# A mixture of experts behind linear attention: routing weights on POOL, and eight routing operations per evacuation

## The chip, the cores and the metric

The kernel runs on one core of one Trainium2 chip. The metric is device time in microseconds (us) of one execution. Engines are called by the profile's names: PE (TensorE), with PEld for its weight loads, DVE (VectorE), ACT (ScalarE), POOL (GpSimd) and SP (SyncE, which only issues transfers here).

## The reference

Two stages. The first is causal linear attention with a decay `lam` per head (batch 4, 8 heads, 768 positions, head size 64), in blocks. Its output is laid out as 3072 tokens of 512 numbers, `x`. The second is a noisy top-2 mixture of 8 experts, cut here to what matters:

```python
logits = x @ w_gate
noise_scale = np.log1p(np.exp(x @ w_noise))
noisy_logits = logits + noise_scale * noise
top2 = np.argpartition(-noisy_logits, 2, axis=1)[:, :2]
top2_l = np.take_along_axis(noisy_logits, top2, axis=1)
top2_l = top2_l - top2_l.max(-1, keepdims=True)
top2_w = np.exp(top2_l)
top2_w /= top2_w.sum(-1, keepdims=True) + 1e-09
for e in range(E):
    for k in range(2):
        mask = top2[:, k] == e
        h = np.maximum(x[mask] @ w1[e], 0.0)
        out[mask] += top2_w[mask, k, None] * (h @ w2[e])
```

So each token has two chosen experts and two weights that sum to one: with `a` the difference of its two largest logits and `e = exp(-a)`, they are 1/(1+e) and e/(1+e).

## The kernel before, in words

**Attention** is a loop of 12 steps `t`, each two chunks of 128 positions of all heads. A step transposes the next step's keys and queries (`trans_k`, `trans_q`), updates the state (`kv`), forms the output (`intra`, `inter`), evacuates it (`evac_o`) and makes the next step's scores (`scores`, whose products DVE masks at L337). `kdecay`, two multiplications on POOL (L322), prepares the keys of step t + 2. One step later the output is multiplied with the gate weights (`products`, L396), stored to `x_tok` in DRAM (`store_x`), and turned into logits (`logits`).

**Routing** is done for three groups of 8 chunks (1024 tokens each). For group `b`, `gate(b)` computes the noisy logits on DVE, the two largest per token (`mx`, L460), their places and a 0/1 matrix `ob` (L472). `weights(b)` fills `rec`, for each token and choice the token's number and its weight; its exponential is a polynomial in `exp_neg` (L92 to L113). `places(b)` counts with PE how many tokens before this one chose the same expert (`count`, L505 to L515, 16 small matmuls on `ob`) and `route(b)` makes of it on DVE the row in the expert's list (`dest`); for the third group `make_order` also ranks the experts. Then 16 scatters per group (`scatter_list`, L548, one per chunk and choice, each 128 rows of 8 bytes) write `rec` into the lists `lst` in DRAM from POOL's queue, each behind a one-element memset (L547).

These are Python generators: every `yield` ends one operation, and the calls `advance(n)` in the loops put up to n operations of the routing at hand between other work; a yielded `"step"` ends such a call early. In attention a step has `advance(4)` behind the query transposes and `advance(16)`, or 10 where it also splits weights, near its end, behind `scatter(SPS)`, which issues up to four of the scatters that are due. The first group's routing is begun at t = 4, the second's at t = 8. At t = 8 `finish(0)` issues what is left of the first group. At t = 10 all scatters left of the first group are issued, then the load of the first list's records (L724) and two gathers of rows of `x_tok` (L728), all on POOL's queue and behind `advance`. After the loop `finish(1)` does the same for the second group, behind the first layer's first block.

**Experts.** Every matmul is done in three products of high and low parts. Expert 0 is worked in three parts of 2, 2 and 3 tiles of 128 tokens (`PARTS0`), so that its first part needs the first group's lists alone, its second the first two groups', its third all. A part is transposes of the gathered rows (`trans_rows`, L737), the first layer in 8 blocks `f` of 12 matmuls (`mm1`, L753), each evacuated by ACT (L759) and DVE (L763), and the second layer, 24 matmuls of 512 columns per tile (`gemm2`, L791). In the first part the loop over `f` calls `advance(FILL1)` after each block, for the third group: f = 0 and 1, whose matmuls were issued earlier, call it too. `advance(50)` follows, up to the `"step"`. `gemm2` of the first tile calls `order_rest`, which is `finish(2)`, before its matmul number `MID`: it issues the rest of the third group's routing, its counts on PE among it, and its 16 scatters. At f = 3 two gathers for the second part stand in POOL's queue; they need the second group's list. The lists and gathers of the third part and of expert 1 follow at the second part's first layer. Experts 1 to 7 run in the order that the counts gave, with their weights loaded (`load_w`) and split (`split_w`, L692 and L693) beside the work of the one before.

A POOL instruction waits in order: what stands behind it in POOL's queue, `kdecay`, scatters and gathers, waits too. The same holds for each of the other engines.

Of the kernel before, what the change touches and what calls it, by code (L numbers as in the profile page):

```python
# [21 lines left out]
FT = mybir.dt.float32  # L22
# [5 lines left out]
OP = mybir.AluOpType  # L28
# [29 lines left out]
MAXOV = 40  # L58
MAXT = 24
FILLA, FILLB = 16, 4  # L60
FILL1 = 5
LOADS = {0: (1, 0), 1: (1, 1), 2: (1, 2), 3: (1, 3), 4: (2, 0), 5: (2, 1), 6: (2, 2), 7: (2, 3)}
SPLITS = {2: (1, 0), 3: (1, 1), 4: (1, 2), 5: (1, 3), 6: (2, 0), 7: (2, 1), 8: (2, 2)}
MID = 16
X1 = ((), (0,), (1,), (2,), (3,), (4,), (5, 6))
WARM = (14, 4, 4, 10)
GX = 10
# [21 lines left out]
    return bass.AP(tensor=ap.tensor, offset=ap.offset + offset, ap=dims)  # L89


def exp_neg(nc, pool, out, a, shape, tag):  # L92

    v = nc.vector
    n = pool.tile(shape, FT, name=tag + "n")
    u = pool.tile(shape, FT, name=tag + "u")
    acc = pool.tile(shape, FT, name=tag + "acc")
    p2 = pool.tile(shape, I32, name=tag + "p2")
    v.tensor_scalar(n, a, -1.0 / math.log(2.0), MAGIC, op0=OP.mult, op1=OP.add)
    yield  # L100
    v.tensor_scalar(n, n, -MAGIC, None, op0=OP.add)
    yield
    v.scalar_tensor_tensor(u, n, math.log(2.0), a, op0=OP.mult, op1=OP.add)
    yield
    v.tensor_scalar(p2, n, 127.0, float(1 << 23), op0=OP.add, op1=OP.mult)
    yield
    v.tensor_scalar(acc, u, EXPC[-1], None, op0=OP.mult)
    yield
    for c in EXPC[-2::-1]:
        v.scalar_tensor_tensor(acc, acc, c, u, op0=OP.add, op1=OP.mult)  # L110
        yield
    v.scalar_tensor_tensor(out, acc, 1.0, p2.bitcast(FT), op0=OP.add, op1=OP.mult)
    yield  # L113


@with_exitstack
def kernel(
# [3 lines left out]
    nc = tc.nc  # L121
# [68 lines left out]
    for i in range(7):  # L190
        n = 1 << i
# [232 lines left out]
    def gate(b):  # L424
        v = nc.vector
        gs = GB[b + 1] - GB[b]
        sh = [128, gs, E]
        t = lambda sh, nm, dt=FT: rp.tile(sh, dt, name=nm)
        pl = PL[b]
        l2 = t([128, gs, 16], "l2")  # L430
        v.tensor_copy(l2, pl[:, :gs, :])
        yield
        zc = t(sh, "zc")
        v.tensor_scalar(zc, l2[:, :, 8:16], 87.0, -87.0, op0=OP.min, op1=OP.max)
        yield
        z = zc.rearrange("p c e -> p (c e)")
        fl = [128, gs * E]
        a = t(fl, "ga")
        v.scalar_tensor_tensor(a, z, -1.0, z, op0=MULT, op1=OP.max)
        yield  # L440
        e = t(fl, "ge")
        yield from exp_neg(nc, rp, e, a, fl, "g")
        acc = t(fl, "glacc")
        v.tensor_scalar(acc, e, LOGC[-1], None, op0=MULT)
        yield
        for c in LOGC[-2::-1]:
            v.scalar_tensor_tensor(acc, acc, c, e, op0=ADD, op1=MULT)
            yield
        acc3 = acc.rearrange("p (c e) -> p c e", e=E)
        v.scalar_tensor_tensor(acc3, l2[:, :, 8:16], 0.0, acc3, op0=OP.max, op1=ADD)  # L450
        yield
        nl = t(sh, "nl")
        v.tensor_mul(nl, acc.rearrange("p (c e) -> p c e", e=E), nz[:, GB[b]:GB[b + 1], :])
        yield
        v.tensor_add(nl, nl, l2[:, :, 0:8])
        yield
        mx = t(sh, "mx")
        mi = t(sh, "mi", U32)
        for c in range(gs):
            v.max(mx[:, c, :], nl[:, c, :])  # L460
            yield
        for c in range(gs):
            v.max_index(mi[:, c, :], mx[:, c, :], nl[:, c, :])
            yield
        ei = t([128, 2, gs], "ei")
        v.tensor_copy(ei.rearrange("p r c -> p c r"), mi[:, :, 0:2])
        yield
        oh = t([128, 2, gs, E], "oh")
        v.tensor_tensor(oh, iota8[:, :, :gs, :], ei[:, :, :, None].to_broadcast([128, 2, gs, E]), op=OP.is_equal)
        yield  # L470
        ob = t(sh, "ob", BF)
        v.tensor_add(ob, oh[:, 0], oh[:, 1])  # L472
        yield
        RT[b] = dict(mx=mx, ei=ei, oh=oh, ob=ob)

    def weights(b):
        v = nc.vector
        gs = GB[b + 1] - GB[b]
        sh = [128, gs, E]
        r = RT[b]  # L480
# [9 lines left out]
        v.tensor_scalar(a, a, 87.0, None, op0=OP.min)  # L490
        yield
        e = t([128, gs], "we")
        yield from exp_neg(nc, rp, e, a, [128, gs], "w")
        s = t([128, gs], "ws")
        v.tensor_scalar(s, e, 1.0, 1e-9, op0=ADD, op1=ADD)
        yield
        v.reciprocal(s, s)
        yield
        recf = rec.bitcast(FT)
        v.tensor_copy(recf[:, :, 0, 1], s)  # L500
        yield
        v.tensor_mul(recf[:, :, 1, 1], e, s)  # L502
        yield

    def count(b):  # L505
        gs = GB[b + 1] - GB[b]
# [67 lines left out]
                                  sub(w, (d * 128 + (h ^ d) * 64) * E, [[E, 64], [256 * E, DB // 2], [1, E]]))  # L574
    keep_warm(WARM[3])

    def merge(*gens):

        gens = list(gens)
        while gens:  # L580
            for x in gens[:]:
                j = next(x, "end")
                if j == "end":
                    gens.remove(x)
                else:
                    yield j

    def places(b):
        yield "step"
        count(b)  # L590
# [3 lines left out]

    def routing(b):
        yield from gate(b)
        yield from merge(weights(b), places(b))
        scatters.extend((b, c, i) for c in range(GB[b + 1] - GB[b]) for i in range(2))
        RT[b]["done"] = True

# [227 lines left out]
    for t in range(NST):  # L828
        u = t + 1
# [278 lines left out]
```

## Time and profile before

| | us |
|---|---|
| three runs | 799.79, 802.74, 807.30 |
| median | 802.74 |
| the profiled execution | 804.76 |
| its span, first to last instruction | 802.9 |
| PE busy | 742.6 (92%), granted clock 0.959 |
| DVE busy | 335.9 (42%) |
| ACT busy | 222.7 (28%) |
| POOL busy | 272.7 (34%) |

The profile has a page and views of one execution's trace. A row of a timeline is: start, duration, engine, line of the kernel, operation, tile written <- tiles read, shape, count, and in brackets how long the engine was idle before it and what ended that. In the row of a group "x48 | 47.2, 982" is 48 instructions, 47.2 us in all, 982 ns each. A row of windows gives a stretch and for each engine its busy time in it with the number of instructions. Spans on POOL are rough. The attention lasts until about 171 us, the first part of expert 0 until about 213, its second until about 250; the rest is the other experts.

### The profile page before, as it was taken

The numbers are of one execution on the slowest core, as the hardware profiler recorded it, in microseconds if no ns is written. First come the engines' busy times: TensorE is split into PE (matmuls) and PEld (weight loads), VectorE is DVE, ScalarE is ACT, GpSimd is POOL, SyncE is SP. The second block draws the span as 40 slices with busy tenths as digits, with TensorE's granted clock in tenths as the row PEclk, the third lists the DMA queues.
The fourth block names the chain that finished last, engine by engine and source line by source line (L and its number), as shares of the span: only waits on it lengthen the run. The fifth ranks groups of instructions, "written<-read, shape, count | busy, mean of one in ns | idle before, by whom it ended". The sixth has DMA issues, their size and how long they took to land. (4 is left out here: it accounts for less than half of the span.)

```text
span 802.9 us, 15437 instructions
## 1 busy us (share of the span) xinstructions
PE 742.6 (92%) x6132; PEld 627.3 (78%) x6132; DVE 335.9 (42%) x796; ACT 222.7 (28%) x381; POOL 272.7 (34%) x399
## 2 busy tenths in 40 slices
PE   5979998784969999999999999999999999999993
PEld 3778877474758889889888888888888888889882
DVE  5435878344412555435243424433352443335210
ACT  0435553232011343214222321322142232214100
POOL 1222115626555145442354234333413433221221
PEclk9899999597979999999999999999999999999997
DMA  7899984111817165344253524333442444240210
GB/s 174 183 279 226 266 231 103 52 56 44 298 50 222 66 172 153 118 145 139 68 144 114 152 82 154 119 118 101 148 133 78 148 134 130 65 129 26 59 53 20
DMA packets 92666, 103.48 MB, mean 129 GB/s; under 512 B 39203, under 2 KB 65315, under 8 KB 92592
## 3 DMA queue, kind: packets, MB, share of 16 engines
q1 hardware_dynamic: 72640, 63.35, 28.8%
q0 software_dynamic: 13136, 36.23, 13.8%
q10 hardware_dynamic: 6816, 2.90, 1.6%
q8 instruction: 49, 0.80, 0.4%
q14 instruction: 25, 0.20, 0.1%
HBM read 77.78 MB, written 25.93 MB: 129 GB/s over the span
## 5 line engine op out<-in xcount | busy, mean ns | idle before, releaser
L753 PE MATMUL pS<-xth,w1h 128*128 128x512 f32 (+3 forms) x544 | 183.6, 338 | 8.5 <-issue 6.3
L753 PE MATMUL pS<-xtl,w1h 128*128 128x512 f32 (+3 forms) x544 | 182.3, 335 | 6.6 <-issue 5.7
L753 PE MATMUL pS<-xth,w1l 128*128 128x512 f32 (+3 forms) x544 | 182.5, 336 | 5.6 <-issue 5.6
L763 DVE SCALAR_TENSOR_TENSOR ht<-pS,ht 128x256 fp32r<-128x256 f32 (+3 forms) x176 | 76.4, 455 | 168.0 <-ACT ht L759 139.5
L810 POOL DMA_INDIRECT out_dram<-ot,rec x46 | 65.3, 1419 | 186.0 <-DVE ot L803 174.8
L791 PE MATMUL pO<-w2h,ht 128*128 128x512 f32 x384 | 126.1, 399 | 0.0
L791 PE MATMUL pKV<-w2h,ht 128*128 128x512 f32 x384 | 125.6, 398 | 0.0
L759 ACT ACTIVATE ht<-pS 128x512 fp32r<-128x512 f32 (+3 forms) x136 | 65.4, 484 | 205.8 <-PE pS L753 159.5
L753 PEld LDWEIGHTS pS<-xth,w1h 128*128 128x128 f32 x544 | 104.4, 192 | 19.0 <-issue 6.4
L753 PEld LDWEIGHTS pS<-xth,w1l 128*128 128x128 f32 x544 | 104.4, 192 | 16.9 <-issue 8.1
L753 PEld LDWEIGHTS pS<-xtl,w1h 128*128 128x128 f32 x544 | 104.4, 192 | 14.4 <-issue 4.4
L739 ACT ACTIVATE xth<-pS 128x512 fp32r<-128x512 f32 (+2 forms) x53 | 29.8, 572 | 205.2 <-PE pS L737 205.0
L791 PEld LDWEIGHTS pO<-w2h,ht 128*128 128x128 f32 x384 | 72.7, 189 | 16.3
L791 PEld LDWEIGHTS pKV<-w2h,ht 128*128 128x128 f32 x384 | 72.3, 188 | 16.3
L791 PE MATMUL pO<-w2l,ht 128*128 128x512 f32 x192 | 76.0, 396 | 0.0
L791 PE MATMUL pKV<-w2l,ht 128*128 128x512 f32 x192 | 75.7, 394 | 0.0
L322 POOL TENSOR_TENSOR kd<-kt,Mk 128x512 f32<-128x512 f32 x24 | 24.8, 1056 | 101.8 <-PE pR L381 57.7
L548 POOL DMA_INDIRECT lst<-rec,dest x48 | 47.2, 982 | 34.6 <-DVE rec L502 24.9
L775 POOL DMA_INDIRECT pv<-out_dram,rec x46 | 47.1, 1025 | 31.0 <-issue 28.0
L728 POOL DMA_INDIRECT xg<-x_tok,rec x46 | 50.1, 1090 | 21.3 <-issue 14.8
L803 DVE SCALAR_TENSOR_TENSOR ot<-pO,rec,pv 128x512 f32<-128x512 f32 x21 | 15.8, 751 | 82.7 <-PE pO L791 82.7
L803 DVE SCALAR_TENSOR_TENSOR ot<-pKV,rec,pv 128x512 f32<-128x512 f32 x21 | 15.8, 751 | 81.4 <-PE pKV L791 81.4
(186 smaller groups left out, 977.1 us busy)
## 6 DMA issues: line engine op xcount, KB each, us to landing
wst<-in_moe_w_dram SPq DMA_DIRECT2D x48, 512.0 KB
wst<-in_moe_w_dram SPq DMA_DIRECT2D x32, 256.0 KB
x_tok<-xc SPq DMA_DIRECT2D x24, 256.0 KB
out_dram<-zero SPq DMA_DIRECT2D x24, 256.0 KB
kt<-in_k_dram SPq DMA_DIRECT2D x11, 512.0 KB
qt<-in_q_dram SPq DMA_DIRECT2D x22, 256.0 KB
vt<-in_v_dram SPq DMA_DIRECT2D x10, 512.0 KB
vt<-in_v_dram ACTq DMA_DIRECT2D x2, 512.0 KB
```

Of the source, the lines that this page charges most:

```text
L322: nc.gpsimd.tensor_mul(kd[:, :, s], kt[:, :, s], mask(s, slice(0, HP), slice(C - 1, C)).to_broadcast([128, HP, 2, D]))
L548: st = nc.gpsimd.indirect_dma_start(out=lst, out_offset=bass.IndirectOffsetOnAxis(ap=r["dest"][:, i, c:c + 1], axis=0), in_=r["rec"][:, c, ...
L728: nc.gpsimd.indirect_dma_start(out=XG[t][:size(e, t)], out_offset=None, in_=x_tok[:rows, :], in_offset=bass.IndirectOffsetOnAxis(ap=REC[e, ...
L739: nc.scalar.activation(hi, p, AF.Copy)
L753: nc.tensor.matmul(p, W1[a][d][:, fs], xt(b, cs)[:, d], start=(d == 0 and i == 0), stop=(d == DB - 1 and i == 2))
L759: nc.scalar.activation(ht(e, 0, f, cs), p, AF.Relu)
L763: nc.vector.scalar_tensor_tensor(ht(e, 1, f, c), p[:, r], 0.0, ht(e, 0, f, c).bitcast(FT), op0=OP.max, op1=SUB)
L775: nc.gpsimd.indirect_dma_start(out=PV[t][:size(e, t), :], out_offset=None, in_=out, in_offset=bass.IndirectOffsetOnAxis(ap=REC[e, t][:, 0: ...
L791: nc.tensor.matmul(p, ht(e, a, f, cs), W2[b][f // 2][:, f % 2, :], start=(i == 0), stop=(i == len(terms) - 1))
L803: nc.vector.scalar_tensor_tensor(o, p, w, pv, op0=MULT, op1=ADD)
L810: st = nc.gpsimd.indirect_dma_start(out=out, out_offset=bass.IndirectOffsetOnAxis(ap=REC[e, t][:, 0:1], axis=0), in_=o, in_offset=None, bo ...
```

## The change

Three things. `weights(b)` is written for POOL instead of DVE, but for the reciprocal, which stays on DVE; POOL has no use of the fused operation with two inputs and a scalar here, so `exp_neg` makes two operations of each such one, in all 25 on POOL for 19 on DVE. `routing` no longer issues weights and places in turn: all of the weights up to the sum are issued at once when the gate is done, then the places, then the reciprocal and the last two operations. And two constants change: `FILL1`, routing operations per block in expert 0's first part, from 5 to 8, and `MID`, the matmul of the first tile's second layer before which `order_rest` is called, from 16 to 6.

```diff
-FILL1 = 5
+FILL1 = 8
...
-MID = 16
+MID = 6
...
-def exp_neg(nc, pool, out, a, shape, tag):
-
-    v = nc.vector
+def exp_neg(v, pool, out, a, shape, tag, fused=True):
+
+    def stt(o, x, c, y, op0, op1):
+        if fused:
+            v.scalar_tensor_tensor(o, x, c, y, op0=op0, op1=op1)
+        else:
+            v.tensor_scalar(o, x, c, None, op0=op0)
+            v.tensor_tensor(o, o, y, op=op1)
+        yield
+
...
-    v.scalar_tensor_tensor(u, n, math.log(2.0), a, op0=OP.mult, op1=OP.add)
-    yield
+    yield from stt(u, n, math.log(2.0), a, OP.mult, OP.add)
...
     for c in EXPC[-2::-1]:
-        v.scalar_tensor_tensor(acc, acc, c, u, op0=OP.add, op1=OP.mult)
-        yield
-    v.scalar_tensor_tensor(out, acc, 1.0, p2.bitcast(FT), op0=OP.add, op1=OP.mult)
-    yield
+        yield from stt(acc, acc, c, u, OP.add, OP.mult)
+    yield from stt(out, acc, 1.0, p2.bitcast(FT), OP.add, OP.mult)
...
-        yield from exp_neg(nc, rp, e, a, fl, "g")
+        yield from exp_neg(v, rp, e, a, fl, "g")
...
     def weights(b):
-        v = nc.vector
+        v = nc.gpsimd
...
-        yield from exp_neg(nc, rp, e, a, [128, gs], "w")
+        yield from exp_neg(v, rp, e, a, [128, gs], "w", fused=False)
         s = t([128, gs], "ws")
         v.tensor_scalar(s, e, 1.0, 1e-9, op0=ADD, op1=ADD)
-        yield
-        v.reciprocal(s, s)
+        yield "sum"
+        nc.vector.reciprocal(s, s)
         yield
         recf = rec.bitcast(FT)
         v.tensor_copy(recf[:, :, 0, 1], s)
-        yield
         v.tensor_mul(recf[:, :, 1, 1], e, s)
-        yield
...
-    def merge(*gens):
-
-        gens = list(gens)
-        while gens:
-            for x in gens[:]:
-                j = next(x, "end")
-                if j == "end":
-                    gens.remove(x)
-                else:
-                    yield j
-
...
     def routing(b):
         yield from gate(b)
-        yield from merge(weights(b), places(b))
+        ws = weights(b)
+        while next(ws) != "sum":
+            pass
+        yield from places(b)
+        yield from ws
         scatters.extend((b, c, i) for c in range(GB[b + 1] - GB[b]) for i in range(2))
         RT[b]["done"] = True
```

## The prediction

> **What bounds the kernel now.** I read the 40 slices of the page first: TensorE (PE) is at 9 tenths in nearly every slice after 260 us, so whatever reaches PE late after that has no room to show, and what is to be won or lost lies where it is thin, at 120 to 160, 180 to 200 and 220 to 240 us. PE's waits over 100 to 245 us (whom it waited for: us in total, times, longest) say of what kind these holes are:
>
> ```profile
> core 0 of [0], span 802.9 us
> ...
> PE pS L753 <- issue: 16.9, 18, 1.8
> PE pS L334 <- issue: 3.2, 6, 1.1
> ...
> PE pS L334 <- DVE qTs L313: 0.8, 1, 0.8
> ```
>
> Hardly any of it is a wait for another engine: "issue" is time in which the profile shows nothing to wait for. The windows (busy time of PE, PEld, DVE, ACT, POOL, then the granted clock, the DMA share and GB/s) put it in place:
>
> ```profile
> 120.00:137.00 17.00, 15.36 (x425) 13.68 (x416) 14.92 (x48) 7.45 (x15) 8.85 (x14) 0.90 0.49 125
> 137.00:154.00 17.00, 11.06 (x66) 4.41 (x59) 3.27 (x12) 0.20 (x1) 12.31 (x23) 0.60 0.03 2
> 154.00:171.00 17.00, 15.26 (x338) 14.16 (x336) 12.37 (x68) 7.99 (x15) 2.74 (x4) 0.90 0.29 97
> 171.00:186.00 15.00, 12.27 (x100) 11.11 (x100) 5.13 (x19) 5.19 (x12) 9.06 (x17) 1.00 0.11 36
> 186.00:198.00 12.00, 2.97 (x12) 2.38 (x12) 3.52 (x14) 0.95 (x3) 7.97 (x15) 0.73 0.02 1
> 198.00:209.00 11.00, 11.00 (x61) 9.34 (x61) 8.73 (x69) 2.82 (x7) 2.21 (x3) 0.82 0.96 340
> 209.00:221.50 12.50, 11.32 (x76) 10.04 (x74) 3.29 (x7) 1.47 (x3) 10.14 (x19) 1.00 0.78 250
> 221.50:232.00 10.50, 3.63 (x13) 2.35 (x13) 0.43 (x1) 0.38 (x1) 6.73 (x13) 0.70 0.02 1
> ```
>
> In 137 to 154, 186 to 198 and 221.5 to 232 us PE gets through 66, 12 and 13 matmuls, DMA moves 1 or 2 GB/s, and POOL is the one engine that works. What POOL does then is its timeline:
>
> ```profile
> 136.65 1.04 POOL L548 DMA_INDIRECT lst<-rec,dest  x1 [0.15 <-issue]
> ...
> 150.75 0.97 POOL L548 DMA_INDIRECT lst<-rec,dest  x1 [0.23 <-issue]
> 154.26 0.59 POOL L724 DMA_DIRECT2D recz<-lst  x1 [2.55 <-DMA lst<-rec,dest]
> 156.37 1.06 POOL L728 DMA_INDIRECT xg<-x_tok,recz  x1 [1.52 <-DMA recz<-lst]
> 157.73 1.01 POOL L728 DMA_INDIRECT xg<-x_tok,recz  x1 [0.30 <-issue]
> 158.74 0.09 POOL L547 MEMSET spacer<- 1x1 f32 x1
> 175.19 1.04 POOL L548 DMA_INDIRECT lst<-rec,dest  x1 [16.36 <-DVE rec L502]
> ...
> 199.52 1.10 POOL L728 DMA_INDIRECT xg<-x_tok,recz  x1 [4.00 <-ACT ht L759]
> ...
> 209.38 1.04 POOL L548 DMA_INDIRECT lst<-rec,dest  x1 [7.34 <-DVE rec L502]
> ```
>
> Each hole is the tail of a run of list scatters: twelve of the first group (136.65 to 151.7, one per 14.10/11 = 1.28 us), sixteen of the second from 175.19, sixteen of the third from 209.38. PE keeps going for some 11 to 12 us of the sixteen and then crawls until about 2.4 us after the last one (175.19 + 16 x 1.28 = 195.6, PE back at 198.0; 209.38 + 20.4 = 229.8, back at 232.0; the twelve: 151.7, back at 153.7). What the crawl is made of the trace doesn't show; that it goes with the scatters, all three times, it does. In 175.2 to 198 PE did 89 matmuls (x100 and x12, less the 23 before 175.2), in 209.4 to 232 some 87. I take it that a run of sixteen lets PE do about 88 and no more, however long these are. The price of a run is then 22.8 us less what 88 matmuls would take, and it matters **when the run starts and which matmuls stand under it.**
>
> **What is waited for in turn.**
>
> ```profile
> 153.72 1.29 DVE L337 TENSOR_TENSOR at<-pS,Mk 128x512 f32<-128x512 f32 x2 [12.10 <-PE pR L396]
> ...
> 156.99 0.64 DVE L460 MAX8 mx<-nl 128x8 f32<-128x8 f32 x8
> ```
>
> ```profile
> 171.77 1.09 PE L737 MATMUL pS<-identf,xg 128*128 128x128 f32 x8
> ...
> 174.65 0.28 PE L753 MATMUL pS<-xth,w1l 128*128 128x256 f32 x1
> 174.77 0.28 PE L753 MATMUL pS<-xth,w1h 128*128 128x256 f32 x1
> ...
> 200.80 0.63 PE L791 MATMUL pO<-w2h,ht 128*128 128x512 f32 x1
> ...
> 212.97 1.03 PE L737 MATMUL pS<-identf,xg 128*128 128x128 f32 x8
> ```
>
> A first-layer matmul of two tiles costs 0.12 us from start to start, the last twelve after the crawl 2.8/12 = 0.23 us (198.0 to 200.80, lower clock), a second-layer one 12.17/48 = 0.25 us with the counts of the third group among them.
>
> **The change, part by part.** Counting yields: `gate` has 45, `weights` had 19, of which 18 vector operations leave DVE per group (the reciprocal stays); POOL gets 25. Of these, two copies need nothing late, 21 form a chain from the maxima (`mx`) to the sum, two follow the reciprocal. All 23 up to the sum are issued at once where the gate ends, ahead of the next scatters.
>
> *Price of the chain.* No such POOL operation is in this trace. Nearest rows:
>
> ```profile
> 1.74 0.19 POOL L234 MEMSET linit<- 128x116 int32 x1
> 1.99 0.15 POOL L235 MEMSET linit<- 128x58 int32 x1
> ...
> L1026 POOL COPY spacer<-ht 1x1 f32<-1x1 f32 x53 | 9.5, 179 | 105.2 <-ACT ht L759 105.1
> ```
>
> The second memset overwrites part of the first and starts 0.25 us behind it; its own 0.15 is the low end, and for the high end I take 0.5, twice that spacing, since every operation takes up what the one before it wrote. I take 0.25, the one spacing of two dependent POOL operations: 21 x 0.25 = 5.3 us (3.2 to 10.5).
> The Trainium skill speaks against the move: GPSIMD Engine Reference, section 3, has VectorE roughly twice as fast for ordinary elementwise work. No run here shows it; with 0.4 us each, twice DVE's spacing, the chain would be an estimated 8.4 us and the sum 3.1 us worse.
>
> *First group.* Its chain runs on POOL while POOL waits for PE (steps t = 6 and 7), covered; without cover it would hold back `kd` for the next step. DVE loses the tail that made PE wait 0.8 for `qTs`: -0.8 (0 to -1.6).
>
> *Second group.* Its gate ends at t = 10, so its chain stands in POOL's queue behind eight of the twelve scatters and ahead of four, of the record load and of both gathers. Eight end 4 x 1.28 = 5.1 us sooner, so PE revives at 148.6 - 0.8 = 147.8, having crawled some 10 matmuls less: -4.0 for PE. The four scatters come later and cost again: the window 120 to 137 has four, and 17.0 - 15.36 = 1.6 idle, half of it the `qTs` wait: +0.9 (0 to 3). PE is then ready for the gathered rows at 171.8 - 0.8 - 4.0 + 0.9 = 167.9. **What is late next is POOL's chain:** `mx` at 157.6 - 5.9 = 151.7, chain to 157.0, four scatters to 162.1, then as before 7.0 us from the last scatter's end (151.7) to the second gather's end (158.7): 169.1; landing as slow as the scatters' 2.5 gives 171.6. So PE starts the transposes at 171.6: nearly all of the 4.8 us is given back to the gathers.
>
> *Run of the second group.* Its records are ready on POOL before that (reciprocal right behind the routing of t = 11, no longer 175.0), so the run starts at 169.4 in place of 175.19, and PE revives at 198.0 - 5.8 = 192.2. Under it fit 88 matmuls: 52 up to the logits, then f = 2 to 4. Left are 36 of the first part instead of 12: 13 x 0.23 + 23 x 0.12 = 5.8, so the second layer starts near 198.0 in place of 200.8: -2.8.
>
> *Eight operations per evacuation.* The 45 yields end in f = 5, the counts go between f = 6 and f = 7, and routing, order and reciprocal are all issued by f = 7. `MID` then finds the routing done and only issues scatters: the counts stand ahead of the whole first tile. Their 16 matmuls (0.5 us) only move. They wait for `ob` behind five gate operations after f = 5's evacuation: f = 6 takes 1.4 us or more, evacuation and five operations about 2.0: +0.5 (0 to 3.4; 3.4 if PE stands at the end of f = 6 when it revives, since two evacuations and 13 operations are still to come).
>
> *Run of the third group.* Gathers end 4 us after the revival (199.52 + 1.36 + 1.01 - 198.0 = 3.9, two gathers spaced as at 156.37): 196.2, chain to 201.5, reciprocal and two POOL operations 0.6: 202.1 in place of 209.38, -7.3. PE revives at 224.7. Under this run stand 34 second-layer matmuls, 8 transposes and 46 first-layer ones in place of 15, 8 and some 64; 18 more of the latter are then left: 18 x 0.12 = 2.2. Net at that point: -7.3 + 2.2 = -5.1, in which the -2.8 + 0.5 are contained.
>
> **Sum.** With 0.25 us for POOL's operations -5.1; rows later are PE-bound, so it stays. The list loads and gathers for the third part start with the scatters' end and come earlier too. The profiled execution took 804.76 (span 802.9 and 1.9 around it), so 799.7; it lies 2.0 above the median of the three runs, 802.74, on whose scale this is 797.6. Own range, 21 x 0.15 to 21 x 0.4 and 0 to 2 for the four scatters: 794.5 to 802.
>
> **Rivals.**
> 1. *The crawl has a fixed length.* PE's first 11 to 12 us under both long runs speak for a time as well as for a count. Moving a run then moves its hole, and only the 0.2 us at the transposes is left: 802.5.
> 2. *POOL's chain is dear.* At 0.4 to 0.5 us an operation every run and gather slips by 3.1 to 5.3 us: 800.7 to 802.9. The rule of the Trainium skill's GPSIMD Engine Reference, section 3, would end here.
> 3. *The crawl is shorter than counted:* PE's hole after eight scatters is filled by other work, the four cost nothing, POOL's operations take 0.15: 797.6 - 2.1 - 0.9 - 2 = 792.6.
> 4. *The counts stop PE (slower).* Mechanism: PE reaches the end of f = 6 during the crawl, as it does now (12 matmuls in 186 to 198 are just f = 6), and then can't pass to f = 7 and the second layer before `ob`. Price 3.4 us, on top of rival 1, whose runs give nothing back: 802.5 + 3.4 = 805.9. It decides as soon as f = 6 is through when PE revives. Against it: the run starts before the transposes, so PE is some 24 matmuls behind.
>
> **How the numbers follow.** The forecast 0.45, rival 1 0.20, rival 2 0.12, rival 3 0.12, rival 4 0.11. A measurement of this kernel tells about 1% (8 us) from no change: faster means under 794.7, slower over 810.8. Faster: all of rival 3 and the lower third of the forecast, 0.26. Slower: half of rival 4 with a dear chain on top and a little of rival 2, 0.08. Same: 0.66. The range 791 to 806 takes in rival 4's own time and rival 3's and leaves out about 2 in 10.
>
> **What would show it.** Right: POOL's 21 operations at about 0.25 us between the second group's `mx` and its last four first-group scatters; eight and four scatters in place of twelve; the runs of sixteen start near 169 and 202 us; PE's issue waits under 100 to 245 us shorter; DVE's `w` rows gone but for the reciprocal. Wrong: PE waiting at L737 for the gathers well past 172 us (chain too dear), at the counts for `ob` by more than 1 us (rival 4), or holes of 10 to 12 us behind runs that start earlier (rival 1).

## The result, and the profile after

The changed kernel takes **813.38 us** (median of 20 executions, 806.42 to 822.78) against 803.40 us for the kernel before on the same chip: ratio **1.0104**, 95% interval 1.0084 to 1.0123. It is slower by one per cent, where 797.6 us had been forecast and the range ended at 806. A second measurement gave 1.0115 (1.0083 to 1.0146). The execution profiled with the first result was a disturbed one (822.78 us), so the rows below are from the second one's profile, of the same kernel.

PE's waits over 100 to 245 us (whom it waited for: us in total, times, longest):

```profile
core 0 of [0], span 815.0 us
...
PE pS L338 <- issue: 6.3, 12, 1.1
PE pS L748 <- issue: 5.2, 4, 2.4
PE pL L511 <- DVE ob L476: 4.9, 1, 4.9
PE pS L748 <- ACT xc L411: 4.7, 1, 4.7
PE pR L400 <- ACT xo L372: 4.6, 1, 4.6
PE pS L748 <- ACT xth L734: 3.6, 1, 3.6
```

Before, most of these waits were "issue" (24.3 of 30.6 us, 16.9 of it at the first layer's matmuls, now L748). Now single long waits for other engines stand beside a smaller issue wait: for the last attention step's output (`xo`), for its copy (`xc`), for the transposed rows (`xth`) and for the counts' matrix (`ob`). The windows place them (PE, PEld, DVE, ACT, POOL, clock, DMA share, GB/s):

```profile
137.00:150.00 13.00, 8.62 (x90) 4.06 (x80) 4.70 (x15) 0.91 (x2) 8.88 (x19) 0.67 0.02 2
150.00:172.70 22.70, 20.02 (x329) 16.46 (x324) 10.22 (x53) 7.06 (x13) 12.04 (x36) 0.81 0.19 60
172.70:195.00 22.30, 10.40 (x80) 8.55 (x71) 1.38 (x2) 2.66 (x5) 16.84 (x31) 0.69 0.06 13
195.00:214.00 19.00, 11.89 (x86) 11.57 (x87) 12.93 (x70) 7.08 (x16) 6.95 (x21) 0.80 0.91 330
```

POOL's timeline shows what the change did there:

```profile
152.93 0.20 POOL L492 TENSOR_TENSOR wa<-mx 128x8 f32<-128x8 f32 x1 [5.34 <-DVE mx L464]
153.21 0.25 POOL L494 TENSOR_SCALAR wa<-wa 128x8 f32<-128x8 f32 x1
153.55 0.20 POOL L106 TENSOR_SCALAR wn<-wa 128x8 f32<-128x8 f32 x1
...
159.01 0.25 POOL L499 TENSOR_SCALAR ws<-we 128x8 f32<-128x8 f32 x1
159.32 0.09 POOL L549 MEMSET spacer<- 1x1 f32 x1
159.58 1.09 POOL L550 DMA_INDIRECT lst<-rec,dest  x1 [0.17 <-issue]
...
163.49 0.96 POOL L550 DMA_INDIRECT lst<-rec,dest  x1 [0.23 <-issue]
167.06 0.59 POOL L719 DMA_DIRECT2D recz<-lst  x1 [2.61 <-DMA lst<-rec,dest]
169.23 1.06 POOL L723 DMA_INDIRECT xg<-x_tok,recz  x1 [1.57 <-DMA recz<-lst]
...
172.66 1.07 POOL L550 DMA_INDIRECT lst<-rec,dest  x1 [0.36 <-POOL spacer L549]
```

The chain is there, 21 operations from 152.93 to 159.26, 0.30 us each (forecast 0.25, bounds 0.15 to 0.5). Eight of the run's twelve scatters precede it, four follow. The second run starts at 172.66, 2.5 us earlier than before. But PE is not where it was. Rows of before (query transposes of the last step but one, products of the last two steps):

```profile
157.91 1.07 PE L306 MATMUL pS<-identf,qt 128*128 128x128 f32 x8
...
164.35 0.64 PE L396 MATMUL pR<-xo,wgn 128*32 128x256 f32 x8
...
171.20 0.64 PE L396 MATMUL pR<-xo,wgn 128*32 128x256 f32 x8 [1.25 <-ACT xo L368]
```

and of after, on to the second layer:

```profile
155.31 1.07 PE L310 MATMUL pS<-identf,qt 128*128 128x128 f32 x8
...
166.59 1.08 PE L400 MATMUL pR<-xo,wgn 128*32 128x256 f32 x8
...
178.11 1.08 PE L400 MATMUL pR<-xo,wgn 128*32 128x256 f32 x8 [4.56 <-ACT xo L372]
179.12 1.97 PE L732 MATMUL pS<-identf,xg 128*128 128x128 f32 x8
184.70 0.58 PE L748 MATMUL pS<-xth,w1h 128*128 128x256 f32 x1 [3.61 <-ACT xth L734]
...
196.11 0.58 PE L748 MATMUL pS<-xth,w1h 128*128 128x256 f32 x1 [4.70 <-ACT xc L411]
...
211.31 0.21 PE L511 MATMUL pL<-ob,lstrict 128*128 128x64 bf16 x1 [4.86 <-DVE ob L476]
...
214.51 0.63 PE L786 MATMUL pO<-w2h,ht 128*128 128x512 f32 x1
```

Milestones of PE, before and after: last attention products (L400) 171.20 and 178.11, so +6.9; first part's transposes 171.77 and 179.12, +7.4; second layer 200.80 and 214.51, +13.7; second part's transposes 212.97 and 226.62, +13.7; third part's 249.17 and 261.01, +11.8; end of the span 802.9 and 815.0, +12.1. From the third part's transposes to the end it is 553.7 us before and 554.0 after: **all is decided before 261 us.** Executions also differ in how they come through the attention (the products that stand at 104.04 us before stand at 105.20 here, in others at 97 to 108), so a few us between two spans are nothing; verdicts below are medians.

### The profile page after: what moved, and what is told of

It is laid out like the page before. It is cut to its first block, busy times and chain, and to the rows that moved or that the text cites. A ratio compares the mean times of both kernels' runs of the same rounds, so it can differ in the third digit from the quotient of the medians.

```text
span 821.0 us, 15456 instructions
## 1 busy us (share of the span) xinstructions
PE 747.0 (91%) x6132; PEld 630.4 (77%) x6132; DVE 329.7 (40%) x742; ACT 223.0 (27%) x381; POOL 288.3 (35%) x474
## 5 line engine op out<-in xcount | busy, mean ns | idle before, releaser
L748 PE MATMUL pS<-xth,w1h 128*128 128x512 f32 (+3 forms) x544 | 183.6, 338 | 14.6 <-ACT xth L734 11.3
L748 PE MATMUL pS<-xth,w1l 128*128 128x512 f32 (+3 forms) x544 | 182.2, 335 | 2.4 <-issue 2.4
L748 PE MATMUL pS<-xtl,w1h 128*128 128x512 f32 (+3 forms) x544 | 182.5, 335 | 2.0 <-issue 1.4
L748 PEld LDWEIGHTS pS<-xth,w1h 128*128 128x128 f32 x544 | 104.5, 192 | 24.0 <-ACT xth L734 12.1
L748 PEld LDWEIGHTS pS<-xtl,w1h 128*128 128x128 f32 x544 | 104.5, 192 | 12.6 <-issue 2.9
L748 PEld LDWEIGHTS pS<-xth,w1l 128*128 128x128 f32 x544 | 104.5, 192 | 10.5 <-issue 1.6
L734 ACT ACTIVATE xth<-pS 128x512 fp32r<-128x512 f32 (+2 forms) x53 | 30.0, 572 | 209.5 <-PE pS L732 202.1
```

Source lines behind the costliest of these rows:

```text
L734: nc.scalar.activation(hi, p, AF.Copy)
L748: nc.tensor.matmul(p, W1[a][d][:, fs], xt(b, cs)[:, d], start=(d == 0 and i == 0), stop=(d == DB - 1 and i == 2))
```

## The experiments

Seven comparisons with the kernel before were made, on several chips, and **they are of two kinds**. In four the kernel before took 803 to 805 us, in three 783 to 785. The profile of before on one of the latter, 779.6 us long, against the one the prediction was made from: 22.8 us from the start of the second run (175.2, there 162.7), first the known kernel's profile,

```profile
175.20:198.00 22.80, 12.43 (x90) 11.52 (x89) 6.84 (x26) 4.53 (x11) 17.02 (x31) 0.86 0.08 24
```

then the same stretch on the other kind of chip:

```profile
162.70:185.50 22.80, 21.07 (x148) 19.11 (x146) 13.93 (x84) 7.46 (x17) 16.90 (x31) 0.93 0.10 25
```

POOL issues the same 16 scatters in the same time, but PE does 148 matmuls, not 90. On that chip PE waits for something else, by its waits over 100 to 245 us:

```profile
core 0 of [0], span 779.6 us
...
PE pS L737 <- DMA xg<-x_tok,recz: 11.4, 6, 4.6
...
PE pS L334 <- issue: 1.4, 1, 1.4
PE pL L509 <- DVE ob L472: 1.4, 2, 1.0
```

There PE waits for gathered rows. I call the first kind *crawling* chips and the second *free* ones; whether the kind belongs to a chip or to a time, the runs don't tell (the first two comparisons on free chips were on the same chip). The changed kernel itself was measured on crawling chips alone; the nearest to it on a free one is weights_alone, below. The expectations were written for the times of the crawling kind (803 before); on the free kind they are read as differences from 783.

### The first four: hold the run, move the chain, one part each (free chip, before 783.15)

Three theories stood at the start. H: the second run now meets the attention's last step and the first part's transposes, and in a run the hand-offs from engine to engine are slow. C: PE stops at the counts for `ob`. G: the second group's chain makes the first part's gathers late.

**late_run**: the second group's reciprocal, and with it the second run, only behind the first part's transposes.

```diff
         yield from places(b)
+        if b == 1:
+            yield "step"
         yield from ws
```

> The changed kernel, but the second group's reciprocal and the two POOL operations behind it are issued where the kernel before issued them, behind the transposes of expert 0's first two tiles; nothing else moves. Theory H (hand-offs): the changed kernel's second run of sixteen scatters starts at 172.2 us while PE is still in the attention's last step, so each hand-off from PE to ACT to DVE and back on the way into the first layer takes 4 to 9 us instead of under one. With the run held back it starts near 177 us, the first layer's matmuls start before 178 in place of 194.9, and the time falls to 803 to 808. Theory C (the third group's counts between f = 6 and f = 7 stop PE, 4.9 us, and its chain on POOL delays the third run): both stay, the time stays at 811 or more. Theory G (gathers late behind the chain): the gathers stay late, so at most 2 us are won.

Measured 795.28 us, 1.0164 (1.0131 to 1.0197). The second run did stand behind the transposes (165.15 against 160.22 us), but H had at most 808 for 803, a ratio of 1.006, so H failed here.

**late_chain**: the second group's chain behind the first part's gathers.

```diff
-        ws = weights(b)
+        ws, ps = weights(b), places(b)
+        if b == 1:
+            yield next(ps)
         while next(ws) != "sum":
             pass
-        yield from places(b)
+        yield from ps
```

> The changed kernel, but the second group's weights on POOL are issued behind the first group's last scatters, its record load and both gathers, so that those come as early as in the kernel before; the run of sixteen still starts as soon as its records are ready. Theory G: the gathers land near 161 us, PE starts the transposes at once, the time falls to about 805. Theory H: the run then starts near 170 us, still ahead of the hand-offs into the first layer, which crawl as in the changed kernel: 809 to 815. Theory C: 811 or more.

Measured 792.80, 1.0122 (1.0094 to 1.0150). PE's wait at the first transposes is 4.3 us, against 9.3 in late_run, but the loss stays, where G had a ratio near 1.002: G failed too.

**fill_mid_alone**: the kernel before with the two constants.

```diff
-FILL1 = 5
+FILL1 = 8
...
-MID = 16
+MID = 6
```

> The kernel before with FILL1 = 8 and MID = 6 alone; all weights on DVE as before. Theory C: PE waits 3 to 5 us for the third group's 0/1 matrix at the counts, and since the third run starts only 3 to 4 us earlier the sum is +0 to +5: 804 to 808. Theory H: the second run keeps its place, so at most 2 us from before: 801 to 806, and the first layer's start keeps its 174 us.

Measured 782.95, 1.0016 (0.9991 to 1.0040): **the constants cost nothing,** although PE does wait 4.8 us at the counts for `ob`, as rival 4 had it: its waits for gathered rows are 6.4 us, against 11.4 in the profile of before on this kind of chip. C is out as the main cause.

**weights_alone**: the changed kernel with the old constants.

```diff
-FILL1 = 8
+FILL1 = 5
...
-MID = 6
+MID = 16
```

> The changed kernel with FILL1 = 5 and MID = 16: weights on POOL and the new order in the routing, without the two constants. Theory H: the second run starts near 172 us as in the changed kernel, so most of the loss stays: 809 to 817. Theory C: no counts between f = 6 and f = 7, so the time falls to 803 to 807.

Measured 790.47, 1.0092 (1.0068 to 1.0117). The loss is there without the constants, so it is in the weights on POOL and the new order, which none of the three theories placed rightly for this chip. Its timeline of POOL gave the next theory:

```profile
193.47 1.05 POOL L723 DMA_INDIRECT xg<-x_tok,recz  x1 [4.51 <-DMA recz<-lst]
194.82 1.02 POOL L723 DMA_INDIRECT xg<-x_tok,recz  x1 [0.31 <-issue]
195.85 0.34 POOL L489 CAST rec<-tokf 128x8 int32<-128x8 f32 x2
...
203.60 1.16 POOL L550 DMA_INDIRECT lst<-rec,dest  x1 [0.40 <-POOL spacer L549]
```

and PE's, later in the same execution:

```profile
227.70 0.40 PE L786 MATMUL pKV<-w2h,ht 128*128 128x512 f32 x1
233.28 1.11 PE L732 MATMUL pS<-identf,xg 128*128 128x128 f32 x4 [5.18 <-DMA xg<-x_tok,recz]
236.80 1.12 PE L732 MATMUL pS<-identf,xg 128*128 128x128 f32 x4 [2.40 <-DMA xg<-x_tok,recz]
```

The third group's chain stands in POOL's queue **behind** the two gathers of the second part, which wait 4.51 us for the list that the second run wrote, and **ahead** of the third run, which so starts 7.8 us after the gathers. In the kernel before, on the same chip, it starts right behind them:

```profile
188.77 1.03 POOL L728 DMA_INDIRECT xg<-x_tok,recz  x1 [0.30 <-issue]
...
190.10 1.04 POOL L548 DMA_INDIRECT lst<-rec,dest  x1 [0.21 <-issue]
```

The third part's rows come with that run, and PE waits for them from 228.10 on (5.18 and 2.40 us in the rows above, 2.1 and 1.8 in the kernel before on that chip).

### Which group's chain, on a free chip (before 783.10)

In **third_back** the third group's weights are DVE's again, with the fused operations, merged with its places as before; in **mid_back** the second group's:

```diff
-        v = nc.gpsimd
+        v = nc.gpsimd if b not in (2,) else nc.vector
...
+        if b in (2,):
+            yield from merge(ws, places(b))
+        else:
+            while next(ws) != "sum":
+                pass
+            yield from places(b)
+            yield from ws
```

with `(1,)` in mid_back.

> The third group's weights go back to VectorE, interleaved with its places as before; the first two groups' stay on POOL, both constants stay. Theory T (what costs is the third group's chain: on POOL it stands behind the two gathers of the second part, which wait for the second run's list, and ahead of the third run of scatters, so the third run starts some 7 us after the gathers instead of right behind them and PE waits at the transposes of the third part): third run starts within 1.5 us of the second gather's end, PE's waits for gathered rows fall to 4 to 9 us from 13 to 20, ratio to before 0.998 to 1.003. Theory M (the second group's chain ahead of the first part's gathers costs): ratio 1.006 to 1.010, the long wait at the first part's transposes near 9 us stays and decides.

> The second group's weights go back to VectorE, interleaved as before; the first and third group's stay on POOL, both constants stay. Theory T: third run still some 7 us behind the gathers, ratio to before 1.006 to 1.012. Theory M: 0.998 to 1.003, the first part's transposes wait 4.6 us instead of 9.4.

third_back: 784.54, **1.0031** (1.0003 to 1.0058). mid_back: 791.13, **1.0106** (1.0079 to 1.0134). On the free chip the third group's chain carries most of the loss, as T said. Two of T's marks were missed: in third_back PE's waits for gathered rows are 10.1 us (4 to 9 had been named), and the third run starts 6.2 us behind the second gather (194.33, it waits for DVE's `rec`), and still PE has no wait at the third part's transposes; of the 10.1 us, 9.7 stand at the first part's, the second chain's share.

**chain_first**: the two gathers of the second part behind f = 5 instead of f = 3, so behind the third chain in POOL's queue.

```diff
-                if f == 3:
-                    for t in range(2, 4):
-                        gather_rows(0, t, GB[2] * C)
                 advance(FILL1)
+                if f == 5:
+                    for t in range(2, 4):
+                        gather_rows(0, t, GB[2] * C)
```

> The kernel after with the two gathers of the second part issued behind the evacuation of f = 5 instead of f = 3, so that the third group's chain stands ahead of them in POOL's queue; nothing else is changed. Theory T: the third run starts within 2 us of the second gather's end, as in the kernel with the two constants alone (0.3 us there), some 6 to 8 us earlier than in the kernel after on the same kind of chip, and the ratio falls from 1.010 to between 0.999 and 1.004. Theory M: the third run moves but the time does not, ratio 1.006 to 1.010. If both chains cost their share, 1.003 to 1.006.

Measured 786.90, 1.0046 (1.0027 to 1.0066), the third run 0.6 us behind the second gather (198.41). About half of the 0.9 to 1.1% seen on this kind of chip with the third chain on POOL comes back by moving two instructions; with the second chain's share left, that is the mixed case.

> The kernel before itself, for its profile on the chip of these runs: T expects its third run within 2 us behind the second gather, and PE's waits for gathered rows at or under 9 us; ratio 1.

That run is the profile of before shown above: 781.38 us, third run 0.3 us behind the second gather; the 11.4 us of waits for rows are above the 9 named.

### The same question on crawling chips (before 804.73, then 804.02)

**after_again** is the changed kernel; its profile is the one in the section on the result.

> The kernel after itself on the kind of chip of the later runs, for an undisturbed profile. Theory T (on POOL the third group's chain of 21 operations stands behind the second part's two gathers and ahead of the third run, about 8 us; the second group's ahead of the first part's gathers, 3 to 5 us): ratio 1.008 to 1.013, third run starts 7 to 8 us behind the second gather, PE's first transposes of the first part wait over 9 us, and PE waits again, 5 to 9 us, at the transposes of the third part. If the loss comes from slowed hand-offs during the second run instead (H), PE's waits are in the attention's last step and at the first matmul behind the transposes, as in the first profile of this kernel, and the third run's distance to its gathers explains nothing.

1.0115, but its waits are not T's. PE waits for `xo` in the attention's last step and behind the transposes, and nowhere for gathered rows; the third run starts 13.0 us behind the second gather's end (204.55 to 217.60) because the gate ends late: from the chain's start (`mx`) at 209.09 to the run it is 8.5 us, in the kernel before 7.9 from its last MAX8's end (201.44) to 209.38. **This is H's picture.** So two runs followed that T had promised would come back:

**both_moved**: late_chain and chain_first together. **first_only**: `merge` for groups 1 and 2, so only the first group's weights on POOL.

> The kernel after with both chains out of the gathers' way: the second group's behind the first part's gathers (as in the run late_chain), the third group's ahead of the second part's gathers (as in the run chain_first). Theory T: both prices are paid back, ratio 0.998 to 1.003. If the second group's chain costs as much behind the gathers as ahead of them (it then delays the second run): 1.004 to 1.007. H: 1.008 to 1.012.

> The weights of the second and third group back on VectorE, interleaved with their places as before; the first group's stay on POOL, and both constants stay. T: the first group's chain has no gather behind it and no run that waits on it closely, ratio 0.999 to 1.003, as with the two constants alone (1.0016). If the first group's chain costs by the delayed decay product, 1.003 to 1.006.

both_moved: 808.73, 1.0065 (1.0042 to 1.0088), outside T and in the range named for a second chain that costs as much behind the gathers as ahead of them. first_only: 807.40, 1.0025 (1.0004 to 1.0046), as expected.

**block_dve**: the changed order with all weights on DVE.

```diff
-        v = nc.gpsimd
+        v = nc.vector
...
-        yield from exp_neg(v, rp, e, a, [128, gs], "w", fused=False)
+        yield from exp_neg(v, rp, e, a, [128, gs], "w")
```

> The kernel after with all weights on VectorE again (the fused operations), but in the changed order: the chain as one block ahead of the counts, not interleaved with the places. Tells POOL's queue from the new order. T: 0.999 to 1.004, third run within 2 us of the second gather. If the new order costs by itself: 1.006 to 1.011.

Measured 812.21, 1.0081 (1.0056 to 1.0105), in the range named for a new order that costs by itself. Not a clean test: the block stands in DVE's queue undivided, ahead of the attention's own work, and PE's last products come at 176.90, 5.7 us later than before. It shows only that the undivided block has a price on DVE as well; what of the loss on POOL is the new order's, no run separates in full, since mid_back and third_back put back order and engine together. It gives DVE's price, too: the chain of 14 fused operations took 2.6 us (172.77 to 175.37), dependent ones 0.21 us from start to start, against POOL's 6.3 us and 0.30.

Then the two groups again, and the wait without the chain:

> The kernel of the run mid_back again (second group's weights on VectorE, third group's on POOL), to be had on a chip where PE stops during the runs of scatters (before near 803 us) if the chip is such a one; on the other kind (before near 783 us) it repeats 1.0106. Theory H2 (where PE stops, the second group's chain costs, because it takes the last four of the first group's twelve scatters out of their run, and PE stops for them and for the second run while the attention's last step and the first part's transposes still stand in it; the third group's chain costs next to nothing, since the third run waits on the gate there): ratio 1.001 to 1.005, transposes of the first part behind 171 to 173 us, the third part's within 4 us of before's 249.2. Theory T (third chain in POOL's queue costs on every chip): 1.007 to 1.012.

> The kernel of the run third_back again (third group's weights on VectorE, second group's on POOL), for the same reason; where before is near 783 us it repeats 1.0031. H2: ratio 1.007 to 1.012 where before is near 803 us, the first transposes at 177 to 181 us and the first matmul of the second layer at 211 to 216. T: 1.000 to 1.005.

mid_back_2: 805.79, **1.0036** (1.0016 to 1.0056). third_back_2: 813.89, **1.0125** (1.0098 to 1.0153). On crawling chips the order is reversed: **the second group's chain carries the loss, and the third's, with the constants, costs 0.4%.** H2's two prices hold here, T's don't, but not all of H2's marks: third_back_2's ratio is just above the 1.007 to 1.012 named, its first transposes come at 174.90 us (177 to 181 named) and its second layer at 210.36 (211 to 216), and mid_back_2's transposes at 168.33 (171 to 173).

**wait_alone**: the kernel before and one tiny POOL copy that waits for the second group's `mx` where the chain would begin.

```diff
+    hold = consts.tile([128, 1], FT, name="hold")
...
         yield from gate(b)
+        if b == 1:
+            nc.gpsimd.tensor_copy(hold, RT[b]["mx"][:, 0, 0:1])
         yield from merge(weights(b), places(b))
```

> The kernel before, all weights on VectorE and both constants as before, with one tiny POOL copy more that reads the second group's mx at the place where the changed kernel's second chain begins: it holds the four scatters behind it for that wait (5.3 us there) without the chain's 6.3 us. H2 on a chip with before near 803 us: about half to all of the second chain's price, ratio 1.004 to 1.010, with a run of 8 and a run of 4. If it is the chain's own time that counts: 0.999 to 1.003. On the other kind of chip (before near 783 us) the split costs nothing by itself and the first gathers are late by the wait only: 0.999 to 1.003.

Measured 801.76, **0.9972** (0.9950 to 0.9995). The scatters do stand as 8 and 4, the copy waits 5.0 us, and the kernel gets no slower, where H2 had 1.004 to 1.010: the split and the wait cost next to nothing by themselves (a gain of another kind that is mixed in here is the subject of tile_alone, below), so H2's account failed. What the changed kernel has beyond this is the chain's own 6.3 us ahead of the four scatters and the gathers, and a reciprocal that no longer waits for DVE's share of the chain, so that gathers are later and the run is earlier.

In the profiles on crawling chips, the place of the first part's transposes against the start of the second run goes with the time from that start to the second layer:

| kernel | transposes after run start | second layer after run start |
|---|---|---|
| before | -3.4 | 25.6 |
| wait_alone | -3.4 | 25.9 |
| tile_alone (below) | -3.4 | 25.7 |
| first_only (new constants) | -3.4 | 29.3 |
| mid_back_2 (new constants) | -3.4 | 30.5 |
| block_dve (new constants) | +0.2 | 32.2 |
| both_moved (new constants) | +2.0 | 37.0 |
| third_back_2 (new constants) | +6.2 | 41.7 |
| after_again (new constants) | +6.5 | 41.8 |

The same profiles place the loss ahead of that. Times of PE in us from the first of the long run's scatters (136.65 in before, 137.37 in after_again):

| kernel | query transposes, last step but one | its products | last products |
|---|---|---|---|
| before | 21.3 | 27.7 | 34.6 |
| wait_alone (8 and 4) | 16.9 | 25.3 | 32.8 |
| block_dve | 20.4 | 27.7 | 33.8 |
| mid_back_2 | 20.8 | 27.3 | 34.1 |
| both_moved | 21.8 | 28.2 | 35.1 |
| third_back_2 (8, chain, 4) | 17.4 | 28.4 | 40.7 |
| after_again (8, chain, 4) | 17.9 | 29.2 | 40.7 |

In all three kernels with the run split, PE comes to the query transposes 3 to 4 us sooner. With a wait alone between the eight and the four, that ends in a gain of 1.8 us; with the chain there as well, in a loss of 6. The chain puts the four scatters 4.3 us behind those transposes (159.58 against 155.31 in after_again; in wait_alone 143.66 against 145.19), and the second run starts before the last products (172.66 against 178.11; in wait_alone 165.12 against 161.13). The new order on DVE (block_dve) and the chain on POOL elsewhere (both_moved) end this stretch within 0.8 us of before.

late_run sets the place that the first of these tables lists, so it was run once more, and wait_alone with it:

> The kernel of the run late_run again (the second group's sum is inverted only behind the transposes of the first part, so that the second run starts behind them). Where PE stops during the runs (before near 803 us), H2 says that the place of the first part's transposes against the start of the second run decides: 6 us behind the start the second layer begins 42 us after it, 3.5 us ahead of it 26 to 30 us after it. It then expects the transposes ahead of the run again, the second layer 26 to 32 us after its start, and a ratio of 1.002 to 1.007 instead of 1.0115. If the chain's 6 us on the way to the gathers cost by themselves: 1.009 to 1.014. On the other kind of chip (before near 783 us) it repeats 1.0164.

> The kernel of the run wait_alone again (before, with the last four of the first group's scatters held for the second group's mx), to see whether 0.997 comes back on this chip: 0.995 to 0.9995 where before is near 803 us; 0.998 to 1.003 where before is near 783 us, since PE does not stop there and a shorter run has nothing to give back.

Both came on a free chip (before 785.06): late_run_2 1.0175 (1.0126 to 1.0225), as there before. **On a crawling chip it stays untried,** so the first table is a correlation over nine kernels, and that the place of the run is the cause is argued, not shown. wait_alone_2: 780.20, 0.9955 (0.9930 to 0.9981), a gain where none had been expected; its copy finds `mx` ready and holds nothing up, and the twelve scatters stand in one run.

**tile_alone** asks where that gain comes from: the kernel before with wait_alone's tile of 4 bytes per partition and a memset of it at the start, no wait.

```diff
+    hold = consts.tile([128, 1], FT, name="hold")
+    nc.gpsimd.memset(hold, 0.0)
```

> The kernel before with the one tile that the run wait_alone added (128 partitions by 4 bytes in SBUF) and a memset of it at the start in place of the copy that reads mx: no wait is added, only what lies behind that tile in SBUF is shifted. In both profiles of wait_alone the first group's products already came 2 to 3 us earlier (30.6 and 31.8 us, elsewhere 33.2 to 34.4), and the loads moved 253 and 263 GB/s between 10 and 15 us (elsewhere 184 to 197). If the shifted layout gives the gain: ratio 0.994 to 0.999, over 240 GB/s between 10 and 15 us. If the held scatters give it: 0.999 to 1.002 and under 200 GB/s.

Measured 800.36 against 803.48: **0.9961** (0.9937 to 0.9985). The tile gives the gain. Windows of before, 10 to 15 us:

```profile
10.00:15.00 5.00, 2.41 (x66) 1.72 (x54) 0.88 (x3) 0.00 (x0) 0.36 (x1) 1.00 0.84 189
```

and of tile_alone:

```profile
10.00:15.00 5.00, 2.02 (x50) 1.33 (x42) 2.60 (x6) 0.00 (x0) 2.09 (x2) 1.00 0.97 233
```

The loads move 233 GB/s instead of 189 there, just under the 240 named. But this stretch doesn't tell the layouts apart: without the tile it is 184 to 229 in the other profiles (229 in both_moved), not 184 to 197. The nine us after it do; before and, below, tile_alone:

```profile
15.00:24.00 9.00, 4.87 (x78) 3.44 (x79) 6.10 (x13) 0.00 (x0) 5.01 (x9) 0.64 1.23 261
```

```profile
15.00:24.00 9.00, 6.84 (x85) 4.75 (x86) 5.25 (x14) 0.00 (x0) 3.62 (x9) 0.51 1.16 311
```

That is 300 to 311 GB/s in the three profiles with the tile and 259 to 264 in all the others, and the first products come at 30.6 to 32.1 us with it, at 33.2 to 34.4 without. Why is open: the tile shifts what lies behind it in SBUF, and no run tried other shifts. As far as these runs go the tile is the one thing tried that beats the kernel before, by about 3 us, and wait_alone's wait, compared with it, costs about +0.1%, within both intervals.

## Why the prediction was wrong, point by point

- **A run of sixteen lets PE do about 88 matmuls and no more: right on crawling chips.** In the 22.8 us from a run's start PE did 90 and 87 before, 83 and 91 in after_again, and 80 to 92 in both long runs of every other kernel profiled there. In the ten profiles on free chips it was 104 to 149: the rule is one of the chip that the prediction's profile came from. That hardly any of PE's waiting before was for another engine is too strong: it was 6.3 of 30.6 us.
- **Price of the chain**: 0.30 us an operation, 6.3 us for 5.3. The Trainium skill's GPSIMD Engine Reference, section 3 (VectorE roughly twice as fast for elementwise work), goes in the right direction: one operation took 0.30 us on POOL and 0.21 on DVE, 1.4 times, and the chain, with its unfused operations, 6.3 us for 2.6, 2.4 times.
- **Second group: the step that failed.** The prediction took 4.8 us from PE ahead of the attention's end (0.8 for `qTs`, 4.0 for the split), gave back 0.9 for the four later scatters, and had PE ready at 167.9 and the transposes at 171.6, waiting only for the gathers. The first half came in part: `mx` was done at 152.9, 4.7 us earlier (forecast 5.9), and the query transposes of the last step but one started 2.6 us earlier (157.91 and 155.31). The rest did not. From these transposes to that step's products it is 6.4 us before (to 164.35) and 11.3 after (to 166.59): with the four later scatters in it this stretch costs **4.8 us more, not 0.9**. And the sum put at nothing that the second run reaches back into the attention: the last step takes 11.5 us instead of 6.9, another **4.7 us**. These 4.8 and 4.7, less the 2.6, are the 6.9 us by which the last products are late. Windows of before and, below, of after, in turn from the four scatters on, behind them, and from the start of the second run:

```profile
153.70:171.20 17.50, 15.56 (x339) 14.47 (x339) 12.65 (x68) 8.14 (x15) 2.74 (x4) 0.89 0.28 94
```

```profile
159.50:166.50 7.00, 4.81 (x86) 3.25 (x78) 1.93 (x4) 1.08 (x2) 4.22 (x7) 0.92 0.03 3
166.50:172.70 6.20, 5.70 (x99) 4.30 (x100) 3.13 (x20) 1.53 (x3) 3.09 (x7) 0.81 0.40 129
172.70:178.10 5.40, 0.85 (x28) 0.61 (x19) 0.00 (x0) 1.08 (x2) 4.52 (x9) 0.77 0.19 52
```

  Before, the attention's last 339 matmuls, small ones, pass in 17.5 us without a scatter among them (clock 0.89). After, 86 of them stand in the seven microseconds of the four scatters, and the last 28 with their hand-off to ACT (`xo`, 4.56 us) in the second run's. The clock goes with it: the eight products of a step take 1.08 us there (granted clock 0.50 at 167 and at 178 us) and 0.64 before (1.00). The price of four was read from PE's idle time in one window, 120 to 137 us, with 425 matmuls in it; it didn't carry over to this place. That the second group's weights carry the loss is shown (1.0125 with them on POOL, 1.0036 without); that they do so by the place of the four scatters and of the second run is read from the profiles, and no run moved these alone.
- **Run of the second group**: started at 172.66 (forecast 169.4), PE was back at 196.1 (192.2). But with transposes 6.5 us behind its start instead of 2.2, the run's matmuls were first the attention's last, then these, so 72 of the first layer's 96 were left when it ended, where 36 had been forecast. Forecast for the second layer 198.0, measured 214.5, in which the 4.9 us of the next point are contained.
- **Eight operations per evacuation**: the mechanism of rival 4 came, PE's wait for `ob` at the counts, with 4.9 us for its 3.4, but where it was tried alone, on a free chip, it cost nothing (1.0016). On a crawling chip the constants were not tried alone; first_only, which has them, is at 1.0025, so at most a small part of the loss is theirs.
- **Run of the third group**: 217.6 for 202.1, late because the gate was. The rule of what stands behind the gathers in POOL's queue, priced there as "gathers 196.2, chain to 201.5", was right in kind: on free chips, where PE isn't held by the runs, it carries most of the cost (1.0106 with it in mid_back, 1.0031 without it in third_back), since before the chain wasn't in that queue at all.
- **The rivals**: none was the case. Rival 2 had the right suspect, the chain on POOL, but put the blame on its price (0.4 to 0.5 us; it was 0.30) and not on its place. Rival 4 had the right sign and mechanism, but not the cause. Rivals 1 and 3 took a run's crawl as their subject, which was the one thing that the forecast had right.

## What to carry to other kernels

An operation moved to an idle engine is queued there: list what stands behind it in that queue and ahead of what it itself waits for, before counting what the old engine gains. Here 21 operations of 0.30 us, moved to take 18 off an engine that was 42% busy, stood once ahead of four scatters and two gathers and once ahead of a run of scatters, and the change cost 1%. And a hole that moves earlier is a gain only if what runs ahead of it has ended by then.

## What the runs showed of the hardware

- The kernel before takes 783 to 785 us in some comparisons and 803 to 805 in others; the difference stands in the runs of scatters of 128 rows of 8 bytes (148 or 90 matmuls in the same 22.8 us). Weights on POOL cost about 1% on both kinds of chip (the changed kernel 1.0104 and 1.0115 on crawling ones, weights_alone 1.0092 on a free one), by different groups (the third's on the free, the second's on the crawling: 1.0106 and 1.0036 for mid_back, 1.0031 and 1.0125 for third_back). What PE lacks in the runs on the crawling chips no trace here shows.
- Dependent operations of 128 x 8 elements start 0.28 to 0.34 us apart on POOL (153.21 to 153.55 for one) and 0.21 apart on DVE.
- With one tile of four bytes per partition more in SBUF the loads between 15 and 24 us were faster by about a sixth (300 to 311 GB/s instead of 259 to 264), and the kernel by 0.4%.
